# Splitting a low-rank sum in its four groups of partitions, and mixing from two copies of V that transfers within SBUF lay out

## The chip, the cores and the metric

The kernel runs on one core of a Trainium2 chip. Its time is the device time in microseconds (us); three runs of the kernel before the change gave 668.37, 668.86 and 669.84, so the median is 668.86 us. One further execution was recorded with a profile; times inside the kernel come from it, counted from its first instruction.

The core has five engines that run their own instruction streams and wait for each other on semaphores: TensorE (PE for its matmuls, PEld for its weight loads), VectorE (DVE), ScalarE (ACT), GpSimd (POOL) and SyncE (SP). SyncE and ScalarE issue transfers (DMA); the transfers themselves run on 16 DMA engines.

## The reference

An attention with decay and a mixer follow one another. There are B = 4 batches, 768 positions, 8 heads of 64 columns, so 512 channels.

```python
for b in range(nb):                        # blocks of 64 positions
    intra = (q_b @ k_b.T * Dmask) @ v_b
    inter = (q_b * lam_pow) @ kv_state
    out_b = intra + inter
    kv_state = lam_block * kv_state + k_dec.T @ v_b
x = out as (B, 768, 512)
h = x.transpose(0, 2, 1) @ U @ V           # U: 768 x 32, V: 32 x 768
u = x + h.transpose(0, 2, 1)
result = u + maximum(u @ w_ch1, 0) @ w_ch2 # 512 -> 2048 -> 512
```

The part that matters here is h. For one batch, P = U^T x is the low-rank sum, 32 rows (the rank) by 512 channels, summed over all 768 positions. Then u = x + V^T P.

## The kernel before

**Precision.** For the matmuls of the mixer, whose operands have the type float32r, the kernel splits an operand into a high part, which keeps the upper bits of the word (a bitwise and with `HI`), and a low part, the rest. A product of two split operands is the sum of the products of their parts. For V and P it is V_high P_high + V_low P_high + V_high P_low + V_low P_low. Since the rank is only 32, several parts lie one above the other in the 128 partitions, in four groups of 32 (`G` = 4, `R` = 32), and one matmul sums over them.

**The work.** A step s handles 128 positions of one batch; a batch has NT = 6 steps, and there are NS = 24. The list `pieces` (lines 637 to 667) writes out by hand in which order the parts of all steps are issued, and thereby the order on each engine. In a step, `prep` transposes q and k of the next step (and lets SyncE load later ones), `scores`, `intra`, `state` and `inter` are the attention's matmuls, and `aside` issues side work (the conversion of U, V and the first weights from 64-bit words), of which ScalarE's part is put off to `late`.

**The low-rank sum.** After the last step of a batch, `low` (L469) computes P in PSUM: group g of partitions holds the columns g*128 to (g+1)*128, so that pp is 128 partitions by 128 columns. The PSUM buffer is that of px, the attention's output. For the batches 0 to 2, ScalarE (L484) and VectorE (L516) then copy the four groups side by side into the 32 partitions of `p_f` (32 x 512), VectorE takes the high part into `p_h` (L519), ScalarE writes it to its places in `p_hl` (`spread`, L527), GpSimd subtracts for the low part (L531) and ScalarE copies that to its second place (`spread_low`, L538). These last three are the pieces `next_of_low`, issued early in the next step. The last batch, in the product stage, goes its own way.

**V.** `v_hl` holds V's parts as high, low, high, low in the four groups. `v_steps` makes them: ScalarE copies the high part to the groups 0 and 2 (L707), VectorE and GpSimd compute the low part in the groups 1 and 3 (L711).

**The mix.** `mix` (L552) does for one step four matmuls of 64 partitions (two groups) each, L559: for each half of the channels, one with P's high part and one with its low part, each in two groups. The mix of step `done` stands in step s = done + 7; the first in step 7. `mixed` (L571) adds x.

**After.** `turn` transposes u, splits it (L628, L629) and keeps it for the products with w_ch1 (`hidden`, L818 and L828) and, after a pass through DRAM, w_ch2 (L951 to L955), which fill the time from 113 us to the end.

**Transfers and their semaphores.** SyncE issues q, k, the weights' words (L279, L140) and the stores of u (L577) in program order, ScalarE v. A transfer is issued when its buffer is free, and when the earlier transfer that signalled on the same one of eight completion semaphores has landed.

## Time and profile before

| | |
|---|---|
| median of three runs | 668.86 us (668.37 to 669.84) |
| profiled execution, its own time | 665.92 us |
| span from its first to its last instruction | 664.1 us |
| granted TensorE clock | full speed throughout |
| attention stage, up to the first product with w_ch1 | 0 to about 113 us |
| products with w_ch1, then with w_ch2 | 113 to 388, 388 to 664 us |
| a step of attention in the middle of a batch | 4.3 us |
| L484 ScalarE copies of pp, 32x128 | 6, 0.256 us each |
| L516 VectorE copies of pp, 32x128 | 6, 0.288 us each |
| L519 VectorE high part, 32x512 | 3, 0.414 us each |
| L527 and L538 ScalarE copies, 32x256 | 12 and 6, 0.40 us each |
| L531 GpSimd low part, 32x256 | 6, 0.73 us (up to 1.02) each |
| L707 ScalarE copies of V's high part, 32x384 | 4, 0.51 us each |
| L711 V's low part, 32x384 | VectorE 2 (0.55 and 0.99 us), GpSimd 2 (1.00 us each) |
| L559 the mix's matmuls | 72, 0.32 us each |

How to read it: a row's time is from the start of an instruction to its end; weight loads overlap with matmuls, and engines work side by side, so busy times do not add up to the span. A line such as "x4" in the timeline joins instructions of the same kind that follow each other; the time given is then that of all of them. The idle time in brackets is that of the engine before the row, with what released it.

### The profile page before, as it was taken

The page shows a single profiled execution, that of the slowest core. Times are in us where ns is not written, and L with a number is a line of the kernel's source. Part 1 is how long each engine was busy: PE and PEld are TensorE (multiplying, and loading weights), DVE is VectorE, ACT ScalarE, POOL GpSimd, SP SyncE. Part 2 cuts the span into 40 slices and gives each one's busy share as a digit, 9 for nine tenths or more (in the row PEclk, how much of TensorE's full clock was granted, in tenths as well). Part 3 has the DMA queues.
Part 4 walks back from the last instruction along what each step waited for, and adds up shares of the span by engine and source line. Part 5 has one row for each costly group of instructions (what it writes and reads, how often), then busy time and mean ns, then how long its engine had stood idle before and what let it go on. Part 6 is the DMA issues. An engine that isn't in the chain of part 4 may idle for free.

```text
span 664.1 us, 13400 instructions
## 1 busy us (share of the span) xinstructions
PE 655.3 (99%) x5242; PEld 538.9 (81%) x5242; DVE 491.0 (74%) x862; ACT 280.2 (42%) x530; POOL 115.7 (17%) x98
## 2 busy tenths in 40 slices
PE   8999999999999999999999999999999999999997
PEld 8888989888888888888888888888888888888886
DVE  5579989969999777777796256786685775775854
ACT  4777886555555444444453122332322322322220
POOL 4466876330000000000000000030120300300300
PEclk9999999999999999999999999999999999999999
DMA  9999982445867655555578899763363363543521
GB/s 225 256 239 248 246 216 96 150 169 171 278 239 255 212 201 203 202 202 204 199 267 290 310 324 399 249 211 106 95 209 104 116 192 95 175 141 96 172 82 63
DMA packets 131776, 131.29 MB, mean 198 GB/s; under 512 B 81346, under 2 KB 89794, under 8 KB 131714
## 3 DMA queue, kind: packets, MB, share of 16 engines
q1 hardware_dynamic: 106592, 124.02, 58.3%
q10 hardware_dynamic: 25122, 6.42, 4.3%
q8 instruction: 41, 0.67, 0.4%
q14 instruction: 21, 0.17, 0.1%
HBM read 80.09 MB, written 50.33 MB: 196 GB/s over the span
## 4 chain that ended last, share of the span: by engine, by line
PE 94%; DMA 2%; DVE 1%; SPq 1%; ACT 1%; issue 1%; POOL 0%; ACTq 0%; DVEq 0%
PE pz L818 27%; PE pz L953 14%; PE pz L951 14%; PE pd L828 14%; PE pd L955 13%; PE px L447 3%; PE pss L406 3%; PE px L458 2%; PE pqk L358 2%; PE pkv L425 1%; SPq L279 1%; DMA kraw<-in_k_dram 1%; PE pp L474 1%; DMA qraw<-in_q_dram 1%; PE pm L559 1%; PE put L590 1%
## 5 line engine op out<-in xcount | busy, mean ns | idle before, releaser
L818 PE MATMUL pz<-u_hl,w 128*128 128x512 f32 x768 | 190.1, 398 | 0.0
L818 PEld LDWEIGHTS pz<-u_hl,w 128*128 128x128 f32 x768 | 144.2, 189 | 35.0 <-ACT r L824 0.3
L953 PE MATMUL pz<-w_hl,m 128*128 128x512 f32 x384 | 151.1, 397 | 0.0
L951 PE MATMUL pz<-w_hl,m 128*128 128x512 f32 x384 | 151.0, 397 | 0.0
L955 PE MATMUL pd<-w_d,m 128*128 128x512 f32 x384 | 149.5, 397 | 0.0
L934 ACT ACTIVATE m<-mt 128x512 fp32r<-128x512 f32 x96 | 60.6, 632 | 196.8 <-PE pd L955 137.8
L935 DVE SCALAR_TENSOR_TENSOR m<-rm,m 128x512 fp32r<-128x512 f32 x96 | 71.4, 746 | 52.5 <-ACT m L934 52.2
L980 POOL TENSOR_TENSOR o<-o,u 128x512 f32<-128x512 f32 x20 | 29.8, 1522 | 447.4 <-DVE o L976 447.4
L833 DVE SCALAR_TENSOR_TENSOR r<-pd,r 128x512 f32<-128x512 f32 x96 | 61.8, 686 | 53.3 <-ACT r L824 43.5
L828 PE MATMUL pd<-u_d,w 128*128 128x512 f32 x384 | 98.6, 397 | 0.0
L824 ACT ACTIVATE r<-pz 128x512 f32<-128x512 f32 x96 | 52.1, 596 | 92.7 <-PE pz L818 92.6
L953 PEld LDWEIGHTS pz<-w_hl,m 128*128 128x128 f32 x384 | 72.4, 189 | 17.6
L951 PEld LDWEIGHTS pz<-w_hl,m 128*128 128x128 f32 x384 | 72.4, 188 | 17.6
L955 PEld LDWEIGHTS pd<-w_d,m 128*128 128x128 f32 x384 | 72.4, 189 | 17.5
L828 PEld LDWEIGHTS pd<-u_d,w 128*128 128x128 f32 x384 | 72.2, 189 | 17.2
L936 DVE SCALAR_TENSOR_TENSOR m<-m 128x512 fp32r<-128x512 f32 x96 | 69.0, 721 | 0.9
L933 DVE TENSOR_SCALAR mt<-rm 128x512 uint32<-128x512 uint32 x96 | 46.1, 481 | 28.5 <-DMA rm<-r_d 28.2
L415 DVE TENSOR_TENSOR sm<-pss,mask 128x512 f32<-128x512 f32 x48 | 30.9, 684 | 8.0 <-PE pss L406 7.6
L212 ACT CAST w<-wt 128x512 fp32r<-128x512 f32 x32 | 19.9, 620 | 30.6 <-DVE wt L209 23.4
L447 PE MATMUL px<-vraw,sm 128*64 128x64 f32 x768 | 27.9, 225 | 2.4 <-ACT x_nat L464 0.7
L447 PEld LDWEIGHTS px<-vraw,sm 128*64 128x64 f32 x768 | 25.0, 138 | 5.4 <-ACT qt L364 1.8
L406 PE MATMUL pss<-qt,kt 64*128 64x128 f32 x384 | 28.9, 291 | 0.0
(96 smaller groups left out, 667.7 us busy)
## 6 DMA issues: line engine op xcount, KB each, us to landing
r_d<-r SPq DMA_DIRECT2D x96, 256.0 KB, 2.4
rm<-r_d SPq DMA_DIRECT2D x96, 256.0 KB, 2.7
words<-in_moe_w_ch_dram SPq DMA_DIRECT2D x30, 512.0 KB, 4.4
w_d<-w SPq DMA_DIRECT2D x16, 768.0 KB, 3.4
w_hl<-w_d SPq DMA_DIRECT2D x16, 512.0 KB, 6.3
u_d<-x_nat SPq DMA_DIRECT2D x24, 256.0 KB, 3.9
u<-u_d SPq DMA_DIRECT2D x24, 256.0 KB, 4.1
qraw<-in_q_dram SPq DMA_DIRECT2D x23, 256.0 KB, 4.2
```

Source lines behind the costliest of these rows:

```text
L406: nc.tensor.matmul(out=pss[:, x, a, :], lhsT=kt[half[x], a, :], rhs=qt[half[x], a, :], start=True, stop=True,)
L447: nc.tensor.matmul(out=px[half[t], x, a, :], lhsT=sm[:, x, a, half[t]], rhs=vr[:, 2 * a + x, :], start=(a == 0), stop=(alone and a == HP - 1),
L818: nc.tensor.matmul(out=acc[g][0], lhsT=w[:, n, ct, :], rhs=uhl[g][:, n, ct, :], start=(ct == 0 and n == 0), stop=(ct == CT - 1 and n == 1),)
L824: nc.scalar.mul(rs[g], acc[g][0], 4096.0 + 1.0)
L828: nc.tensor.matmul(out=acc[g][1], lhsT=w[:, 2, ct, :], rhs=ud[g][:, ct, :], start=(ct == 0), stop=(ct == CT - 1),)
L833: nc.vector.scalar_tensor_tensor(rs[g], acc[g][1], 4096.0, rs[g], ALU.mult, ALU.add)
L934: nc.scalar.activation(out=m[:, 0], in_=t, func=AF.Relu)
L935: nc.vector.scalar_tensor_tensor(m[:, 1], r, 0.0, hi, ALU.max, ALU.subtract)
L936: nc.vector.scalar_tensor_tensor(m[:, 2], hi, E, low, ALU.mult, ALU.subtract)
L951: nc.tensor.matmul(out=pz, lhsT=m[:, 0, cols], rhs=hl[:, 0], start=first, stop=False)
L953: nc.tensor.matmul(out=pz, lhsT=m[:, 1, cols], rhs=hl[:, 1], start=False, stop=end)
L955: nc.tensor.matmul(out=pd, lhsT=m[:, 2, cols], rhs=dd, start=first, stop=end)
```

## The change

*Low-rank sum.* For the batches 0 to 2, one VectorE copy takes pp as it lies, 128 partitions by 128 columns, to SBUF, and one operation takes the high part. ScalarE then copies the high part of each group to its place (four copies of 32x128), and GpSimd subtracts for the low part of each group (four of 32x128). Nothing is stored twice: `p_hl` becomes a tile of its own with 256 columns. Its groups are: high part of the columns 0 to 255, low part of the same, high part of the columns 256 to 511, low part of the same. The third piece of `next_of_low` is gone for these batches.

*V.* Since P's parts lie only once, V lies in two orders: copy 0 has high, low, high, low in the four groups, copy 1 low, high, low, high. ScalarE writes the high part to group 0 of copy 0, GpSimd the low part to group 1 of copy 0, and six transfers within SBUF, issued by SyncE at the beginning of step 6, before the loads of that step's `prep`, fill the six others (32 partitions by 768 columns of 4 bytes each, 96 KB).

*Mix.* A mix remains four matmuls of 64 partitions by 256 columns; the two that add up now use the two copies of V and the same columns of `p_hl`. The last batch keeps its P in the part of V's second copy that is no longer read by then, and multiplies with copy 0.

*Room.* The one-row tile with lam moves into a part of the tile `blank`, and two constants into `small`.

```diff
@@ -287,11 +287,12 @@
 
     assert G == 4
     vp = w1_pool.tile([P, 3, C], F32R, tag="w1", name="vp").rearrange("p n c -> p (n c)")
-    v_hl, p_hl = vp[:, 0:S], vp[:, S : S + C]
+    v_hl = vp.rearrange("p (n c) -> p n c", n=2)
+    p_hl = consts.tile([P, 2 * P], F32R, name="p_hl")
 
 
     ident = keep.tile([P, P], FP32, name="ident")
-    small = consts.tile([P, 16], FP32, name="small")
+    small = consts.tile([P, 18], FP32, name="small")
     zeros = small[:, 0:1]
 
     mask = consts.tile([P, 2, HP, P], FP32, name="mask")
@@ -464,7 +465,7 @@
         nc.scalar.copy(xs[s].rearrange("p (a x e) -> p x a e", a=HP, x=2), px)
         del st[s]
 
-    pps, others = {}, {}
+    pps = {}
 
     def low(b):
 
@@ -479,17 +480,15 @@
         if b == B - 1:
             pps[b] = pp
             return
-        pps[b] = rows_f = tmp("p_f")[0:R]
-        for g in range(2):
-            nc.scalar.copy(rows_f[:, g * P : (g + 1) * P], pp[g * R : (g + 1) * R])
-        others[b] = pp
+        pps[b] = pp
 
     def low_rows(b):
 
-        pp, t = pps.pop(b), tmp("p_h")[0:R]
+        pp = pps.pop(b)
         own = [(slice(g * R, (g + 1) * R), slice(g * P, (g + 1) * P)) for g in range(G)]
         if b == B - 1:
-            h, h2, l, l2 = (p_hl[g * R : (g + 1) * R] for g in range(G))
+            t = tmp("p_h")[0:R]
+            h, h2, l, l2 = (v_hl[g * R : (g + 1) * R, 1, 0:C] for g in range(G))
             for rows, cols in own:
                 nc.vector.tensor_scalar(
                     t[:, cols].bitcast(U32), pp[rows].bitcast(U32), HI, None, ALU.bitwise_and
@@ -511,33 +510,26 @@
             pps[b] = [spread, low_part, spread_low]
             return
 
-        rows_f, pp = pp, others.pop(b)
-        for g in range(2, G):
-            nc.vector.tensor_copy(
-                out=rows_f[:, g * P : (g + 1) * P], in_=pp[g * R : (g + 1) * R]
-            )
-        nc.vector.tensor_scalar(t.bitcast(U32), rows_f.bitcast(U32), HI, None, ALU.bitwise_and)
-        wide = [slice(x * 2 * P, (x + 1) * 2 * P) for x in range(2)]
+        whole, t = tmp("p_f")[:, 0:P], tmp("p_h")[:, 0:P]
+        nc.vector.tensor_copy(out=whole, in_=pp)
+        nc.vector.tensor_scalar(t.bitcast(U32), whole.bitcast(U32), HI, None, ALU.bitwise_and)
 
         def place(g, low):
-            return p_hl[g * R : (g + 1) * R, wide[low]]
-
-        def spread():
+            n = 2 * (g // 2) + low
+            return p_hl[n * R : (n + 1) * R, (g % 2) * P : (g % 2 + 1) * P]
+
+        def high_part():
             for g in range(G):
-                nc.scalar.copy(place(g, 0), t[:, wide[g // 2]])
+                nc.scalar.copy(place(g, 0), t[g * R : (g + 1) * R])
 
         def low_part():
-            for x in range(2):
+            for g in range(G):
+                rows = slice(g * R, (g + 1) * R)
                 nc.gpsimd.tensor_tensor(
-                    out=place(2 * x, 1), in0=rows_f[:, wide[x]], in1=t[:, wide[x]],
-                    op=ALU.subtract,
-                )
-
-        def spread_low():
-            for x in range(2):
-                nc.scalar.copy(place(2 * x + 1, 1), place(2 * x, 1).bitcast(FP32))
-
-        pps[b] = [spread, low_part, spread_low]
+                    out=place(g, 1), in0=whole[rows], in1=t[rows], op=ALU.subtract
+                )
+
+        pps[b] = [high_part, low_part]
 
     def next_of_low(b):
         pps[b].pop(0)()
@@ -551,19 +543,18 @@
 
     def mix(s):
         b, c = divmod(s, NT)
-        weights = v_hl[:, c * P : (c + 1) * P]
+        weights = v_hl[:, :, c * P : (c + 1) * P]
         if b < B - 1:
             pm = both_halves(s)[:, :, 2 * P :]
-            for low in range(2):
+            for n in range(2):
                 for x in range(2):
                     nc.tensor.matmul(
-                        out=pm[:, x], lhsT=weights[half[x]],
-                        rhs=p_hl[half[x], low * 2 * P : (low + 1) * 2 * P],
-                        start=(low == 0), stop=(low == 1),
+                        out=pm[:, x], lhsT=weights[half[x], n], rhs=p_hl[half[x]],
+                        start=(n == 0), stop=(n == 1),
                     )
             return
         pu = bank([P, C], "pu", "b2")
-        nc.tensor.matmul(out=pu, lhsT=weights, rhs=p_hl, start=True, stop=True)
+        nc.tensor.matmul(out=pu, lhsT=weights[:, 0], rhs=v_hl[:, 1, 0:C], start=True, stop=True)
         nc.vector.tensor_tensor(out=xs[s], in0=pu, in1=xs[s], op=ALU.add)
 
     def mixed(s):
@@ -642,7 +633,7 @@
         turns = done > 0 and (done - 1) // TG < FG
         mixes = 0 <= done < NS - NT - 1
         rows = c == 0 and b > 0
-        step = [("prep", s + 1)] * more
+        step = [("spread_v", s)] * (s == NT) + [("prep", s + 1)] * more
         step += [("turn", done - 1)] * turns + [("mix", done)] * mixes
         step += [("mix", done + 1)] * (not more)
         step += [("next_of_low", b - 1)] * rows + [("next_of_low", b - 1)] * rows
@@ -652,7 +643,6 @@
         step += [("turned", done - 2)] * (done > 1 and c == 1)
         step += [("split", done - 1)] * turns
         step += [("mixed", done)] * mixes + [("mixed", done + 1)] * (not more)
-        step += [("next_of_low", b - 1)] * rows
         both = [("intra", s), ("state", s)]
         step += (both if s > NT else both[::-1]) + [("next_v", s), ("inter", s)]
         step += [("late", s)] * (s < 2 or s in (NT - 1, NT))
@@ -689,11 +679,10 @@
                 st["v"] = wconv.tile([P, C], FP32, tag="wf", name="vf")[0 : 2 * R, 0:SH]
             return st["v"]
 
-        def parts(gs):
+        def parts(g):
             for half in range(2):
                 rows, cols = slice(half * R, (half + 1) * R), slice(half * SH, (half + 1) * SH)
-                for g in gs:
-                    yield v_hl[g * R : (g + 1) * R, cols], rows
+                yield v_hl[g * R : (g + 1) * R, 0, cols], rows
 
         def five():
             st["t"] = t = wconv.tile([P, C], FP32, tag="wt", name="vt")[0 : 2 * R, 0:SH]
@@ -703,18 +692,28 @@
             on_scalar(high)
 
         def high():
-            for out, rows in parts((0, 2)):
+            for out, rows in parts(0):
                 nc.scalar.copy(out, st["t"][rows])
 
-        def low(g, engine):
-            for out, rows in parts((g,)):
-                engine.tensor_tensor(
+        def low():
+            for out, rows in parts(1):
+                nc.gpsimd.tensor_tensor(
                     out=out, in0=st["v"][rows], in1=st["t"][rows], op=ALU.subtract
                 )
 
+        def spread():
+            whole = v_hl.bitcast(FP32)
+            for g, n in ((2, 0), (1, 1), (3, 1), (3, 0), (0, 1), (2, 1)):
+                source = (g + n) % 2
+                nc.sync.dma_start(
+                    out=whole[g * R : (g + 1) * R, n],
+                    in_=whole[source * R : (source + 1) * R, 0],
+                )
+
+        run["spread_v"] = lambda s: spread()
         halves = [moe_V[:, half * SH : (half + 1) * SH] for half in range(2)]
         return weight_steps(dst, halves, SH, 2 * R, in_parts=True) + [
-            five, lambda: low(1, nc.vector), lambda: low(3, nc.gpsimd),
+            five, low,
         ]
 
 
@@ -724,7 +723,7 @@
     side = {}
     for steps, at in (
         (u_side, (-1, 1, 1, 2, 2)),
-        (v_steps(), (0, 0, 3, 3, 4, 4, 4, 5, 5)),
+        (v_steps(), (0, 0, 3, 3, 4, 4, 4, 5)),
         (w1_steps(0, True), (3, 4, 5, 6, 8, 9, 10, 11, 13, 14, 15)),
         (w1_steps(1, True, True), (8, 9, 10, 11, 16, 17, 19, 20, 21, 22, 23, NS)),
     ):
@@ -745,11 +744,11 @@
 
     ordered = ctx.enter_context(ExitStack())
     ordered.enter_context(tc.manual_schedule())
-    lam_row = consts.tile([1, H + P], FP32, name="lam_row")
-    blank = x_pool.tile([P, C], FP32, tag="x", name="blank")[:, 0:P]
+    blank = x_pool.tile([P, C], FP32, tag="x", name="blank")
+    lam_row, blank = blank[0:1, P : P + H + P], blank[:, 0:P]
     nc.vector.memset(blank, 0.0)
     nc.vector.memset(lam_row[:, H:], 1.0)
-    set_ends(vp[:, S + C : S + C + 2].bitcast(FP32))
+    set_ends(small[:, 16:18])
     nc.scalar.dma_start(out=lam_row[:, 0:H], in_=lam.unsqueeze(0))
     load_next("q", nc.sync)
     load_next("k", nc.scalar)
```

## The prediction

> **What bounds the kernel now.** I read the page first, for the engine that sets the time.
>
> ```profile
> span 664.1 us, 13400 instructions
> ...
> PE 655.3 (99%) x5242; PEld 538.9 (81%) x5242; DVE 491.0 (74%) x862; ACT 280.2 (42%) x530; POOL 115.7 (17%) x98
> ...
> PE 94%; DMA 2%; DVE 1%; SPq 1%; ACT 1%; issue 1%; POOL 0%; ACTq 0%; DVEq 0%
> ```
>
> TensorE carries 94% of the chain that ended last. The change touches only the attention stage (up to 113 us) and leaves the number and shape of matmuls as they are, so it can give or take only stretches in which TensorE stands still there. The table by stage finds them (columns: stretch, its length, then busy us and count of PE, PEld, DVE, ACT, POOL, clock, DMA share, GB/s).
>
> ```profile
> 33.00:41.00 8.00, 7.20 (x172) 6.15 (x172) 6.22 (x11) 6.88 (x17) 5.60 (x7) 1.00 0.96 226
> ...
> 60.00:67.00 7.00, 6.75 (x174) 6.00 (x172) 6.07 (x13) 5.29 (x13) 3.99 (x5) 1.00 0.88 220
> ...
> 88.00:94.00 6.00, 5.81 (x154) 5.17 (x154) 5.00 (x10) 4.40 (x12) 3.78 (x4) 1.00 0.75 186
> ...
> 142.00:388.00 246.00, 246.00 (x1052) 197.87 (x1051) 185.61 (x334) 113.75 (x198) 1.30 (x1) 1.00 0.66 230
> ```
>
> After 113 us there is no TensorE gap until 388, so time won or lost before 113 should reach the end one to one. The three short stretches are where a batch's low-rank sum is split. There I read the timeline; in brackets is how long the engine stood idle before, and what ended it. First batch, weight loads and ScalarE:
>
> ```profile
> 37.15 1.66 ACT L527 CAST vp<-p_h 32x256 fp32r<-32x256 f32 x4
> 38.83 0.83 ACT L538 CAST vp<-vp 32x256 fp32r<-32x256 f32 x2
> 39.29 0.18 PEld L559 LDWEIGHTS pm<-vp 64*128 64x128 f32 x1 [0.18 <-ACT vp L538]
> 39.69 0.58 ACT L464 COPY x_nat<-px 128x512 f32<-128x512 f32 x1
> 39.71 0.18 PEld L559 LDWEIGHTS pm<-vp 64*128 64x128 f32 x1 [0.24 <-ACT vp L538]
> ```
>
> The first mix waits for the last of ScalarE's copies, and the next step's attention product, whose weight load starts at 40.32 after 0.43 us idle, waits for x_nat, which stood behind those copies. Second and third batch:
>
> ```profile
> 62.94 0.59 DVE L516 COPY p_f<-pp 32x128 f32<-32x128 f32 x2 [0.79 <-PE pqk L358]
> 63.60 1.04 PEld L447 LDWEIGHTS px<-vraw,sm 128*64 128x64 f32 x32 [0.36 <-ACT qt L364]
> 65.94 0.42 DVE L431 COPY kv<-pkv 128x256 f32<-128x256 f32 x1
> 66.41 0.33 PEld L358 LDWEIGHTS pqk<-ident,qraw 64*128 64x128 f32 x8 [0.26 <-DVE kv L431]
> ```
>
> ```profile
> 90.80 1.04 PEld L447 LDWEIGHTS px<-vraw,sm 128*64 128x64 f32 x32 [0.30 <-issue]
> 91.73 0.58 PEld L425 LDWEIGHTS pkv<-vraw,ks 128*64 128x64 f32 x16
> 92.38 0.97 PEld L406 LDWEIGHTS pss<-qt,kt 64*128 64x128 f32 x16
> 93.61 0.33 PEld L358 LDWEIGHTS pqk<-ident,qraw 64*128 64x128 f32 x8 [0.26 <-DVE kv L431]
> ```
>
> The 0.36 is put down to qt, but px shares its PSUM buffer with pp, and L516, the last reader of pp, ended at 63.53, 0.07 before the weight load; in the third batch it ended at 90.73, 0.07 before 90.80. So I read both as waits for L516. The 0.26 is a wait for kv, which stands on VectorE behind L516, L519 and three operations on u.
>
> **What the Trainium skill says.** "VectorE: DVE Perf Modes", The perf-mode tier table: fp32 tensor_scalar from SBUF runs at two elements a cycle; with the roughly 150 cycles of start that the page gives beside its modes, 512 columns make 406 cycles, 0.42 us. The trace has 0.414 for L519, so I use it for 128 columns: 214 cycles, 0.22 us. "SBUF — State Buffer", Door 1: 32 partitions reach 8 of 16 DMA ports, 189 GB/s measured at 1 MiB; 96 KB would take 0.52 us, an estimate. Here the two V loads of the same shape landed 0.37 us apart, in a full queue. "DMA: Bandwidth & Descriptors", Anatomy: about 2 us fixed per transfer. In this trace the quickest are the last stores (1.8 us, 128 KB) and a first q load (2.4 us); no transfer within SBUF is in it.
>
> **The change part by part.**
>
> *Low-rank sum, three batches.* ScalarE loses two copies of 0.26 (L484), four of 0.415 (L527) and two of 0.41 (L538), and gains four of 32x128. 32x384 takes 0.51 and 32x256 0.40, so 128 columns less are 0.10, and 32x128 costs 0.30, about 1.25 for four: 3.0 becomes 1.25. VectorE: 0.59 and 0.41 become one copy of 128x128 (0.29: the 32x128 copy's time, since 64x384 at 0.35 against 128x512 at 0.41 shows that columns count) and 0.22. GpSimd: two of 0.73 become four of 0.45 (1.00 for 384 columns, 0.73 for 256, so 0.27 per 128): 0.4 us more. Cover: qs, the next thing on GpSimd, is read a step of 4.3 us later; without it the 0.4 would be paid.
>
> Second batch: VectorE copies pp as soon as it is done and its engine free (62.27), ending at 62.6, before the mix's last weight load ends (63.24): the 0.36 goes. p_h is done at 62.85, the first operation on u waits for its transposes (63.2), kv comes 0.8 earlier: the 0.26 goes. What is late next is nothing: scores and kt stand ready. Third batch the same, 0.30 and 0.26. Together 1.18 us. The mix now waits on GpSimd directly; low parts there can start when the previous batch's last mix has read p_hl (63.45) and end at 65.4; the mix stands at 66.6.
>
> *First batch.* High copies end at 38.4 instead of 39.66 and x_nat at 39.0; qt and kt follow, so the 0.18, 0.24 and 0.43 (0.85 together) have no ScalarE cause left. The scores' mask on VectorE (38.64, two of 0.65) is ready for the product at 39.3.
>
> *V.* ScalarE's four copies (2.07) become two, VectorE's two subtractions at 36.23 (1.55) go, GpSimd keeps two. All lay beside TensorE work: nothing on the path. The rows that were computed in place now come by six transfers on SyncE, ahead of the next q, k and weight loads.
>
> ```profile
> 30.60 1.44 SPq L279 DMA_DIRECT2D kraw<-in_k_dram  x1
> 31.40 0.38 ACTq L279 DMA_DIRECT2D vraw<-in_v_dram  x1
> 32.09 1.37 SPq L140 DMA_DIRECT2D words<-in_moe_w_ch_dram  x1
> ...
> 35.73 0.37 SPq L279 DMA_DIRECT2D qraw<-in_q_dram  x1
> ```
>
> SyncE idles from 33.46 to 35.73. The first three transfers wait for V's high copies (33.6), the fourth for GpSimd (34.26); at 0.4 us each, four are issued by about 35.3. In the compiled order each transfer also waits for the earlier one that used its completion semaphore, one of eight in turn: the fifth waits for the k load of 30.60, which the trace has landing at 37.04, the sixth for the v load of 31.40 (36.14). So the fifth goes at 37.1 and the sixth at 37.45. With nothing else on SyncE's queue (DMA moved 57 to 75 GB/s from 36 to 37) I take 2.05 us, between the 1.8 and the 2.4 above: the sixth lands at 39.5. The mix (38.86) needs the fifth for its third and the sixth for its fourth matmul. Fourth weight load 39.55 instead of 39.71, attention product 39.75 instead of 40.32: 0.57 of the 0.85 is won. Bounds: 1.8 us gives 0.8; 4.5 us, the median of a k load under load here, lands at 41.95 and loses 1.9.
>
> Behind them q goes at 37.9 instead of 35.73, k at 38.3, the weights at 38.8 (36.78). Each is read at least two steps, some 8 us, later and takes 4.2 to 4.5 to land; SyncE waited for TensorE again at 43.98, so it has caught up by then. Without that cover q would delay a step by 2.
>
> *Moves of lam_row and the two constants, last batch's rows in V's second copy:* same instructions in the same places; nothing.
>
> Sum: 0.57 + 0.62 + 0.56 = 1.75 us. On the profiled execution, 665.92 with a span of 664.1 and 1.8 around it, that makes 664.2 and 662.35. The median of the runs, 668.86, is 2.9 above it; I take the difference off that: 667.1.
>
> **Rivals.** *Late spread, slower.* At the first mix the sixth transfer takes as long as a load in this stage does. Break-even with the 1.18 of the later batches is an attention product at 41.5, a landing at 41.3, 3.9 us after issue. At 4.5 us the net is 0.6 slower (669.5), at the 6.8 of the slowest k load 3 slower (671.8). For: the queue's share is 0.96 in this stretch, and fewer ports. Against: SyncE's own block empties the queue. 0.15.
>
> *Half a gain.* The 0.36 and 0.30 belong to what the profile names, or an instruction-fetch wait ("issue", 0.66 at 35.43) returns with the loads now bunched at 38 to 41: 0.7 to 1.1 won, 668.0. For: bracketed names. Against: the 0.07 us in both batches. 0.27.
>
> *Whole gain.* The k load lands earlier and the first mix waits for nothing: 0.85 + 1.18 and a little, 666.6. 0.13.
>
> The forecast itself: 0.45, its own range 666.6 to 667.6.
>
> **Numbers.** 0.2% (1.3 us, below 667.5) is about what a measurement tells from no change. Faster: most of the forecast (0.42) and the whole gain, 0.55. Same: 0.03 of the forecast, half a gain, little of the late spread: 0.31. Slower: 0.14. The range 665.9 to 669.6 takes in all but the late spread's tail and part of the whole gain's.
>
> **What would show it.** After: no idle before L447's weight load in the steps after a pp, none before pqk for kv; six transfers issued between 33.6 and 37.9 with a gap before the fifth; the first mix's fourth weight load between 39.2 and 40, released by a transfer. It is wrong if that load stands after 41, if the low parts on GpSimd take over 3 us, or if the time won by 113 us is lost before 388.

## The result, and the profile after

The changed kernel takes 670.62 us, the median of 20 runs (668.16 to 673.84). The kernel before, run beside it, takes 668.85 us (666.62 to 671.15). The ratio is 1.0030, with an interval of 1.0017 to 1.0043: the change makes the kernel about 1.8 us slower. The forecast was 667.1 us, 1.75 us faster, with a range up to 669.6.

The page of the changed kernel: span, busy time of each engine, and the chain that ended last.

```profile
span 668.0 us, 13401 instructions
...
PE 657.0 (98%) x5242; PEld 540.9 (81%) x5242; DVE 487.8 (73%) x857; ACT 273.8 (41%) x516; POOL 115.8 (17%) x104
...
PE 96%; DMA 1%; issue 1%; DVE 1%; ACT 0%; POOL 0%; ACTq 0%; DVEq 0%; POOLq 0%
```

The other engines changed as the diff says: five VectorE and fourteen ScalarE instructions fewer, six on GpSimd more. TensorE is busy 1.7 us longer with the same 5242 matmuls, the first sign that some of them ran slower. The table by stage (columns as in the prediction: stretch, length, then busy us and count of PE, PEld, DVE, ACT, POOL, clock, DMA share, GB/s):

```profile
33.00:41.00 8.00, 5.37 (x141) 4.70 (x132) 3.28 (x7) 5.17 (x14) 6.21 (x8) 1.00 0.89 217
41.00:60.00 19.00, 18.44 (x480) 17.30 (x481) 13.84 (x24) 11.13 (x27) 9.44 (x8) 0.91 1.00 246
...
88.00:94.00 6.00, 6.00 (x178) 5.41 (x176) 5.21 (x10) 3.60 (x8) 3.59 (x3) 1.00 0.98 252
142.00:388.00 246.00, 246.00 (x1054) 197.84 (x1053) 184.35 (x331) 114.52 (x198) 2.60 (x2) 1.00 0.67 231
```

In the third batch (88 to 94) TensorE has no gap left, as predicted. In the first batch (33 to 41) it is busy for 5.37 us instead of 7.20, and in the stretch behind it the mean granted clock is 0.91. From 142 to 388 TensorE is busy throughout in both kernels. The timeline around the first mix, from SyncE's issues (SPq) and TensorE:

```profile
32.48 2.83 SPq L140 DMA_DIRECT2D words<-in_moe_w_ch_dram  x1
...
35.40 4.37 SPq L708 DMA_DIRECT2D vp<-vp  x6
...
38.23 0.19 PEld L551 LDWEIGHTS pm<-p_hl,vp 64*128 64x128 f32 x1
...
41.53 0.74 PEld L551 LDWEIGHTS pm<-p_hl,vp 64*128 64x128 f32 x3 [3.11 <-issue]
41.56 1.00 PE L551 MATMUL pm<-p_hl,vp 64*128 64x256 f32 x3 [2.94 <-DMA vp<-vp]
42.49 1.78 PEld L448 LDWEIGHTS px<-vraw,sm 128*64 128x64 f32 x32 [0.22 <-issue]
42.50 1.97 PE L448 MATMUL px<-vraw,sm 128*64 128x64 f32 x32
```

The first of the four mix matmuls needs no transferred rows and starts at 38.26. The second needs the first and the fourth transfer, of which the fourth landed at 41.32, and stands until 41.53: the transfers, not ScalarE's copies, now hold the mix. (The brackets of the weight loads name "issue" here and GpSimd in other runs below; the landings tell which transfer it was.) Behind it the product px takes 1.97 us, where the same 32 matmuls take 1.15 us in the other steps. The two windows that the profile's clock record marks:

```profile
38.20:41.61 3.41, 0.47 (x12) 0.30 (x6) 1.10 (x2) 2.29 (x7) 2.27 (x3) 1.00 0.83 215
41.61:45.02 3.41, 3.41 (x51) 3.19 (x51) 0.69 (x1) 0.00 (x0) 0.00 (x0) 0.50 1.05 250
```

TensorE was idle for 2.9 of 3.41 us, and in the next 3.41 us it was granted half its clock. The kernel before had no such stretch before its last 0.2 us.

To compare executions I take three segments from the starts of weight loads: from one batch's low-rank sum (pp) to the next, and from the third to the first product with w_ch1. In the kernel before they are 27.74, 27.26 and 25.67 us. The table gives the difference to these in the one profiled execution, and the ratio of the runs' times to those of the kernel before, run beside them. (The ratio is an estimate from all runs, and differs by up to 0.6 parts in a thousand from the quotient of the two medians.) The runs are described below.

| | ratio and 95% interval | span | pp 1 to 2 | pp 2 to 3 | pp 3 to product |
|---|---|---|---|---|---|
| changed kernel | 1.0030 (1.0017 to 1.0043) | 668.0 | +3.61 | +0.37 | −0.29 |
| e1 first mix reads no V | 0.9989 (0.9974 to 1.0003) | 664.3 | +0.32 | −0.15 | −0.29 |
| e2 no transfers | 0.9978 (0.9966 to 0.9989) | 662.0 | −1.47 | −0.83 | −0.30 |
| e3 words later | 1.0026 (1.0015 to 1.0037) | 665.9 | +1.78 | −0.13 | −0.30 |
| e4 wait filled | 1.0024 (1.0013 to 1.0035) | 667.7 | +2.51 | +0.93 | −0.31 |
| e5 four transfers | 1.0025 (1.0009 to 1.0041) | 668.1 | −0.03 | +0.35 | −0.29 |
| e10 the same again | 1.0026 (1.0012 to 1.0041) | 666.5 | +2.66 | −0.06 | −0.30 |
| e6 mix moved | 0.9995 (0.9982 to 1.0009) | 663.8 | −0.17 | −0.84 | −0.30 |
| e7 moved, words later | 0.9982 (0.9968 to 0.9995) | 663.8 | −0.88 | −0.84 | −0.30 |
| e11 the same again | 0.9989 (0.9975 to 1.0002) | 663.4 | +0.21 | −0.84 | −0.29 |
| e8 all three | 0.9996 (0.9985 to 1.0007) | 664.9 | −0.37 | +1.35 | −0.30 |
| e9 V a step earlier | 1.0030 (1.0013 to 1.0046) | 667.9 | −1.06 | +0.80 | −0.30 |
| e12 before, words later | 1.0004 (0.9992 to 1.0016) | 666.8 | −0.10 | +2.30 | 0.00 |

A span is one execution. The last row shows how far one can stand from the median: e12 is 2.7 us longer than the kernel before in the profile, and not told from it in 22 runs. The profiled execution of the changed kernel is nearly 4 us longer, where the medians differ by 1.8. Where the two differ, the ratio counts, and the profile only tells the place.

### The profile page after: what moved, and what is told of

Same layout as the page of the kernel before. It is cut to its first block, busy times and chain, and to the rows that moved or that the text cites. A ratio compares the mean times of both kernels' runs of the same rounds, so it can differ in the third digit from the quotient of the medians.

```text
span 668.0 us, 13401 instructions
## 1 busy us (share of the span) xinstructions
PE 657.0 (98%) x5242; PEld 540.9 (81%) x5242; DVE 487.8 (73%) x857; ACT 273.8 (41%) x516; POOL 115.8 (17%) x104
## 4 chain that ended last, share of the span: by engine, by line
PE 96%; DMA 1%; issue 1%; DVE 1%; ACT 0%; POOL 0%; ACTq 0%; DVEq 0%; POOLq 0%
PE pz L817 27%; PE pz L952 13%; PE pd L827 13%; PE pz L950 13%; PE pd L954 13%; PE px L448 4%; PE pss L407 4%; PE px L459 2%; PE pqk L359 2%; PE pkv L426 1%; PE pp L475 1%; PE pm L551 1%; DMA kraw<-in_k_dram 1%; PE pm L599 1%; PE put L581 1%
## 5 line engine op out<-in xcount | busy, mean ns | idle before, releaser
L416 DVE TENSOR_TENSOR sm<-pss,mask 128x512 f32<-128x512 f32 x48 | 30.9, 684 | 10.6 <-PE pss L407 10.6
L448 PE MATMUL px<-vraw,sm 128*64 128x64 f32 x768 | 29.5, 232 | 1.8 <-issue 0.9
```

The lines of the kernel that those rows point to most:

```text
L448: nc.tensor.matmul(out=px[half[t], x, a, :], lhsT=sm[:, x, a, half[t]], rhs=vr[:, 2 * a + x, :], start=(a == 0), stop=(alone and a == HP - 1),
```

## The experiments

Theory A: the loss is the wait for late transfers at the first mix, and the half clock behind it. Theory B: the loss is the transfers' traffic, the loads that they push back, or the split on GpSimd, wherever the mix stands.

**e1, the first mix reads no V.** The first step's mix takes `p_hl` as its weights, so the right addend of that step is left out; the transfers are issued all the same.

```diff
-                        out=pm[:, x], lhsT=weights[half[x], n], rhs=p_hl[half[x]],
+                        out=pm[:, x], lhsT=p_hl[half[x], 0:P] if s == 0 else weights[half[x], n], rhs=p_hl[half[x]],
```

> The changed kernel, but the first mix (step 0 only) takes the low-rank sum itself as weights in place of V, so that it waits for no transfer; the six transfers stay as they are, and V is first needed a step of 4.3 us later. What step 0 adds is therefore left out. Theory A (the wait for the late transfers is the loss: 3.1 us of idle TensorE and about 1.3 us of half clock behind it, together 4.4): about 666.2 us against 670.6 of the change, and below the kernel before by 2 to 2.7. Theory B (the transfers cost by their traffic, by pushing other loads back, or the split on GpSimd costs): not below the kernel before, 668.9 or more.

Measured: 0.9989. The wait and the half clock are gone, and with them 4 parts in a thousand. But a new wait stands two steps later. Timeline of e1, VectorE and TensorE:

```profile
46.30 0.43 DVE L160 TENSOR_SCALAR sc<-words 128x512 uint32<-128x512 uint32 x1 [0.74 <-DMA words<-in_moe_w_ch_dram]
...
46.64 1.53 DVE L149 TENSOR_SCALAR m<-words 128x512 uint32<-128x512 uint32 x1
...
48.09 1.27 DVE L416 TENSOR_TENSOR sm<-pss,mask 128x512 f32<-128x512 f32 x2
...
48.84 1.13 PEld L448 LDWEIGHTS px<-vraw,sm 128*64 128x64 f32 x32 [1.57 <-ACT kt L365]
```

The words of the weights, pushed back behind the six transfers, landed at 46.28. VectorE's conversion of the words waits for them (0.74 us), the mask of the scores (L416) follows it in VectorE's program, and the attention product, which needs the mask, waits 1.57 us. The bracket names kt, but kt had ended at 48.10, while the first of the two mask operations, 0.68 us each, ended at about 48.77, just ahead of px. Not all of this is the words' lateness: VectorE stood idle for 0.74 us, and then the conversion's second instruction (L149) took 1.53 us, where it takes 0.41 in the kernel before, in the changed kernel and in e6. A GpSimd instruction of 1.28 us began just ahead of it, at 46.61; whether that stretched it, no run here shows. So B is partly right: a pushed-back load can start a wait of 1.57 us, but only when the first wait no longer hides it.

**e2, no transfers.** V's tile is zeroed at the start and six of its eight blocks are left out; everything else is the changed kernel.

```diff
-        run["spread_v"] = lambda s: spread()
+        run["spread_v"] = lambda s: None
...
+    nc.gpsimd.memset(vp.bitcast(FP32), 0.0)
```

> The changed kernel without the six transfers; V's tile is set to zero at the start on an idle GpSimd, so six of the eight blocks of V's two copies are left out of the sum. Theory A: as the run with the first mix freed, 666.2 within 0.5 us. Theory B in the form of traffic: at least 1 us below that run, as the waits for nothing that the profile shows (0.71 and 0.60 us at 67 and 77 us) go with the transfers. B in the form of the split: 669 or more here too.

Measured: 0.9978, the segments −1.47, −0.83 and −0.30. Without the transfers the split, the copies and the mix from two orders gain 2.2 parts in a thousand, 1.5 us, near what the prediction said of them. Taking out the transfers takes out the whole loss, so it is not in the split, and GpSimd's four parts cost nothing that shows. The median is 0.6 us below that of e1, more than A allowed (0.5) and less than B's traffic asked for (1); the two intervals overlap.

**e3, the words behind the transfers.** One fetch of words on SyncE moves from step 5 to step 6, so that it no longer stands ahead of the transfers.

```diff
-        (w1_steps(0, True), (3, 4, 5, 6, 8, 9, 10, 11, 13, 14, 15)),
+        (w1_steps(0, True), (3, 4, 6, 6, 8, 9, 10, 11, 13, 14, 15)),
```

> The changed kernel, but the weights' words that SyncE issues just ahead of the transfers (2.8 us of its time, until 35.3) are issued behind them. Theory A: first transfer at 33.3 instead of 35.4, sixth issued at about 37.3 when the k load has landed, landed by 40.2 instead of 41.9; TensorE idle 1.7 instead of 3.1 us, no half clock: 668 us, between the kernel before and 667. Theory B: 670.6, as the transfers are the same.

Measured: 1.0026. The transfers are issued from 33.50 to 38.26 instead of 35.40 to 39.76 and the last lands at 40.14 instead of 41.88. Weight loads of the first mix in e3:

```profile
39.02 0.18 PEld L551 LDWEIGHTS pm<-p_hl,vp 64*128 64x128 f32 x1 [0.85 <-POOL qs L391]
...
39.89 0.18 PEld L551 LDWEIGHTS pm<-p_hl,vp 64*128 64x128 f32 x1 [0.68 <-DMA vp<-vp]
40.24 0.18 PEld L551 LDWEIGHTS pm<-p_hl,vp 64*128 64x128 f32 x1 [0.17 <-issue]
```

The wait falls from 3.11 to 1.70 us, which is 1.4 of the 1.8 us won in this segment. The first bracket names GpSimd, but the fourth transfer landed at 38.81, 0.21 us ahead of that weight load. The half clock is there again, from 41.65 on. The ratio can't be told from that of the changed kernel, although the landing and the wait came out as A expected. Even with SyncE free in time the transfers are not back in time, since each takes 2.5 to 3.8 us from the start of its issue to its landing, and the six issues 4.8 us together.

**e4, the wait filled.** Eight 128x128 matmuls of the identity with itself go ahead of the first mix, into a part of its PSUM buffer that nothing reads.

```diff
+            for i in range(8 * (s == 0)):
+                nc.tensor.matmul(
+                    out=both_halves(s)[:, 0, 0:P], lhsT=ident, rhs=ident, start=True, stop=True
+                )
```

> The changed kernel with eight matmuls of no use (128x128, into a part of the mix's PSUM buffer that is not read) ahead of the first mix, which fill most of TensorE's wait of 3.1 us. They can gain nothing by themselves. If the wait costs more than its own length because the granted clock halves behind it (3.4 us at half clock, attention products 1.97 instead of 1.15): about 1.3 us less than the change, 669.3, and no stretch at half clock. If the clock is not part of the loss: 670.6 or more.

Measured: 1.0024, no stretch of half clock. Timeline of e4:

```profile
38.65 2.05 PE L550 MATMUL pm<-ident 128*128 128x128 f32 x16
...
41.68 0.31 PEld L555 LDWEIGHTS pm<-p_hl,vp 64*128 64x128 f32 x2 [0.87 <-POOL qs L391]
...
42.49 1.15 PE L448 MATMUL px<-vraw,sm 128*64 128x64 f32 x32
```

px stands at 42.49, as in the changed kernel (42.50), but takes 1.15 us, and the next scores start 2.17 us after it instead of 3.30. So the half clock cost 1.1 us in that execution. The times of the runs don't show this gain: the ratios differ by 0.6 parts in a thousand, well inside the intervals, and the medians, against the kernel before, not at all (1.9 and 1.8 us slower). How much of the loss is the half clock is thus open.

That the stretch comes with a wait can be seen in the mean granted clock of each run. A stretch of 3.41 us at half clock takes 0.0026 off the mean (an estimate: half of 3.41 over 668), so a run that has one should show 0.997 or less. Of the changed kernel's 20 runs 13 do, with a median of 671.0 us; the other seven have 669.6, but a run with a longer wait may have both. Of the runs of the kernel before for which the record gives the clock, 1 of 200 does. In e4 it is none of 20, in e1, e2, e8 and e11 none either, in e7 and e12 1 of 22 each; in e3 7 of 17, in e5 and e10 6 and 9 of 22, in e9 9 of 11 (in the profiles of e5 and e9 the wait and the stretch lie earlier, between 20 and 29 us).

**e5 and e10, four transfers.** Two of the four carry 64 partitions, the bytes are the same.

```diff
-            for g, n in ((2, 0), (1, 1), (3, 1), (3, 0), (0, 1), (2, 1)):
-                source = (g + n) % 2
+            for g, n, source, count in ((2, 0, 0, 2), (1, 1, 0, 2), (0, 1, 1, 1), (3, 1, 0, 1)):
                 nc.sync.dma_start(
-                    out=whole[g * R : (g + 1) * R, n],
-                    in_=whole[source * R : (source + 1) * R, 0],
+                    out=whole[g * R : (g + count) * R, n],
+                    in_=whole[source * R : (source + count) * R, 0],
                 )
```

> The changed kernel, with the six transfers of 32 partitions made four by letting two of them carry 64 partitions (the same bytes). If the time of a transfer's issue and its landing count per transfer (theory A), two issues of 0.7 us fall away, the last lands near 40.6 instead of 41.88, the first mix waits some 1.2 us less, and the ratio to the kernel before falls from 1.003 to about 1.001 (to 0.999 if the stretch of half clock goes too). If the bytes count (theory B), or 64 partitions take longer to land, the wait stays near 3 us and the ratio stays at 1.003.

Measured: 1.0025. The profiled execution had lost 3.4 us ahead of the change, most of it to one wait of 2.77 us that ended at 23.2 and the half clock behind it; as the mix stood later for that reason, the transfers were nearly in time for it (0.61 us of wait). That says nothing on an ordinary execution. The same kernel again:

> The version with four transfers once more, since the profiled execution of its first run lost 3.4 us to a stretch of half clock at 24.6 us, ahead of the change, and so does not show its wait at the first mix. Theory A: in an execution without that early loss the last transfer lands some 1.2 us earlier than with six, and the first mix still waits 1.5 to 2 us; ratio 1.001 to 1.0025. Theory B: the wait is the 3 us of the changed kernel, and the ratio 1.003.

Measured: 1.0026. Weight loads of the first mix in e10:

```profile
38.90 0.18 PEld L551 LDWEIGHTS pm<-p_hl,vp 64*128 64x128 f32 x1 [0.75 <-POOL qs L391]
...
40.78 0.30 PEld L551 LDWEIGHTS pm<-p_hl,vp 64*128 64x128 f32 x2 [1.70 <-issue]
```

The wait is 2.45 us instead of 3.11, so 0.66 of the 1.2 us expected was won: there are two issues fewer, but one of the four took 1.95 us, and landing took 3.2 to 5.0 us from the issue instead of 2.7 to 3.8. The half clock is there again, from 41.49. The ratio doesn't tell this from six transfers.

**e6, the first mix moved.** Mix and addition of the first step go behind the attention products of the same step (2.3 us of TensorE work); nothing else is changed.

```diff
-        step += [("turn", done - 1)] * turns + [("mix", done)] * mixes
+        step += [("turn", done - 1)] * turns + [("mix", done)] * (mixes and done > 0)
...
-        step += [("mixed", done)] * mixes + [("mixed", done + 1)] * (not more)
+        step += [("mixed", done)] * (mixes and done > 0) + [("mixed", done + 1)] * (not more)
...
         step += (both if s > NT else both[::-1]) + [("next_v", s), ("inter", s)]
+        step += [("mix", 0), ("mixed", 0)] * (done == 0)
```

> The changed kernel, with the first mix alone moved behind the attention products of its own step, so that 2.4 us of TensorE work stand between the transposes and it; transfers and loads as in the changed kernel. Theory A (the loss is the wait for the late transfers and the half clock behind it): the wait shrinks from 3.1 to some 0.7 to 0.9 us, no half clock, 3.5 us won, ratio about 0.997 to 0.998. Theory B (the loads pushed back by the transfers cost as much by themselves): the scores' mask of the next step waits for the pushed-back words as it did when the first mix read no transfer, 1.5 us of it come back, ratio 0.999 to 1.000.

Measured: 0.9995, 3.5 parts in a thousand (2.3 us) below the changed kernel, with intervals that do not overlap. Timeline of e6:

```profile
34.03 5.10 SPq L709 DMA_DIRECT2D vp<-vp  x6
...
42.41 0.30 PEld L551 LDWEIGHTS pm<-p_hl,vp 64*128 64x128 f32 x4
```

The last transfer landed at 41.51, the mix started at 42.41 and waited for nothing; this execution has no half clock. Transfers and loads are all there and only their reader stands later, so the wait at the first mix, with what follows it, made up the loss against the kernel before. The ratio itself lies in the range that B had asked for, but not for B's reason: the conversion of the words no longer delays the mask as it did in e1 (VectorE reaches it at 47.32, after the words have landed at 45.85). What keeps e6 from the 0.9978 of e2 is in part open. The wait for x_nat (see e7) is in it, and 4 of the 22 runs still have a mean clock of 0.997 or less, with a median of 668.7 us against 665.9 for the other 18; where these lose it, no trace shows.

**e7 and e11, mix moved and words later.**

> First mix moved behind its step's attention products, and the words' fetch of step 5 moved to step 6, behind the transfers, so that the transfers are issued from 33.5 on as predicted and land by 40.1. Theory A: no wait is left at the first mix (it stands near 40.9), span about 2 us below the kernel before, ratio 0.997. Theory B: the words land later still (near 46.5), VectorE's conversion waits for them and holds the scores' mask back, ratio 0.999 to 1.001.

Measured: 0.9982. Timeline of e7, SyncE and weight loads:

```profile
34.69 3.77 SPq L709 DMA_DIRECT2D vp<-vp  x6
...
40.25 1.12 PEld L448 LDWEIGHTS px<-vraw,sm 128*64 128x64 f32 x32 [0.46 <-ACT x_nat L465]
...
42.54 0.30 PEld L551 LDWEIGHTS pm<-p_hl,vp 64*128 64x128 f32 x4
```

The mix runs its four matmuls in one go. What is late next is px, for x_nat, by 0.46 us: the kernel before had a wait of 0.43 us for it here, and with the mix gone from in front of px nothing hides it. The ratio lies between what A and B expected. Once more:

> The version with the first mix moved and the words behind the transfers once more, to see whether it beats the kernel before. Theory A: ratio 0.997 to 0.999 with an upper end below 1. Theory B: 0.9995 to 1.001, the first result having been luck.

Measured: 0.9989, with an interval that just reaches 1. The two ratios say 1.2 and 0.7 us faster than the kernel before, the medians 0.9 and 0.4; one of the two intervals excludes no change, the other doesn't. And since this version carries the words' new place, the kernel before got it alone (e12, the diff of e3 on the old kernel):

> The kernel before, with nothing but the words' fetch of step 5 moved to step 6. If what the moved-mix version wins over the kernel before comes from the change's split of the sum and the transfers once they are in time (theory A), this makes no difference: ratio 0.9995 to 1.0005. If it comes from fetching the words later, with the change having no part in it (theory B), ratio 0.998 to 0.999. If the words land too late for VectorE's conversion here too, ratio 1.001 or more.

Measured: 1.0004 (0.9992 to 1.0016). The words' place is worth nothing that shows by itself. The kernel before was not run with its first mix moved. Its own mix waits 0.18 and 0.24 us for ScalarE's copies, so up to 0.4 us of what e7 and e11 win could come from the move alone; that is not tested.

**e8, all three.** Four transfers, mix moved, words later.

> Four transfers, first mix moved, words behind the transfers. If both parts of the loss are understood, this comes to what the kernel without transfers showed: ratio 0.998, span 662.0 to 662.5, no half clock, no wait at the first mix; SyncE is free for q, k and words some 1 to 1.5 us earlier than with six transfers, so the scores' mask waits at most 0.5 us for words. If the transfers cost by their traffic in a way that neither the count nor the place touches, it stays at 0.9995 to 1.001.

Measured: 0.9996. No wait at the first mix and no half clock, as expected, but no better than with six transfers: the ratio lies where the expectation put a cost of the traffic itself, and that cost stays neither shown nor excluded. In its profile the second batch is 1.35 us longer, with four waits of 0.29 to 0.48 us that are put down to nothing ("issue"). Such waits come without the change too: e12 has four in its second batch, from 0.32 to 1.15 us. So I don't count them for or against four transfers.

**e9, V a step earlier.** Conversion, copies and transfers of V move ahead by a step; the mix stays.

```diff
-        (v_steps(), (0, 0, 3, 3, 4, 4, 4, 5)),
+        (v_steps(), (0, 0, 2, 2, 3, 3, 3, 4)),
...
-        step = [("spread_v", s)] * (s == NT) + [("prep", s + 1)] * more
+        step = [("spread_v", s)] * (s == NT - 1) + [("prep", s + 1)] * more
```

> The changed kernel, with the conversion of V, its two copies and subtractions and the six transfers each one step (4.3 us) earlier; the first mix stays where it is, and so do the words. Theory A (the transfers come too late for the first mix, and nothing else is wrong with them): they are issued from about 30 on and have landed by 37, ahead of the mix near 38.5; no wait there, no half clock, pp to pp in the first batch 0.5 to 1.5 us shorter than before, ratio 0.997 to 0.999. Theory B (their traffic and the loads behind them cost as much wherever they stand): q and k of the next steps land later and the scores of step 6 or 7 wait 1 to 2 us, ratio 1.001 to 1.003.

Measured: 1.0030, outside what A expected and inside what B did. Timeline of e9, in step 2 and at the first mix:

```profile
22.25 0.35 DVE L160 TENSOR_SCALAR sc<-words 64x384 uint32<-64x384 uint32 x1 [1.49 <-DMA words<-in_moe_V_dram]
...
22.90 1.50 DVE L178 SCALAR_TENSOR_TENSOR m<-words,m 64x384 f32<-64x384 uint32 x1
...
24.33 1.27 DVE L416 TENSOR_TENSOR sm<-pss,mask 128x512 f32<-128x512 f32 x2
...
25.12 1.82 PEld L448 LDWEIGHTS px<-vraw,sm 128*64 128x64 f32 x32 [3.55 <-ACT sc L168]
...
41.89 0.31 PEld L551 LDWEIGHTS pm<-p_hl,vp 64*128 64x128 f32 x4
```

The first mix waits for nothing, and its segment is 1.06 us shorter than before: what A says of that place is right. But the loss came back elsewhere. V's own words had not landed when VectorE reached them (1.49 us idle), one instruction of the conversion took 1.50 us where it takes 0.55 in the kernel before, the mask stood behind both, and TensorE waited 3.55 us, with half clock from 24.8. It is the chain of e1 again, and not that of q and k which B named.

## Why the prediction was wrong

**The step that failed: the landing of the sixth transfer in the part on V.** I let SyncE be free at 33.46, took 0.4 us for each issue and 2.05 us from issue to landing, and made the fifth wait for a k load. All three terms were too small, and the wait that I put in cost nothing. From the view of the line that issues them:

```profile
L708 SPq DMA_DIRECT2D vp<-vp x6: 540/594/1165, 35.4 to 39.2; - x6
...
DMA to landing us min/median/max: 2.7/3.1/3.8
```

- SyncE was free at 35.30. The words' issue ahead of the transfers took 2.83 us instead of 1.37. That an issue's time varies was to be read from the profile before: its three issues of w_ch1 words near this place took 1.84, 0.97 and 1.37 us.
- The six issues took 4.37 us instead of some 2.4. I had argued that SyncE's queue would be empty when they came; it was not: v, q, k and words landed at 35.55, 36.37, 37.28 and 38.19 (the share of the DMA engines was 0.89 from 33 to 41).
- Landing took 2.7 to 3.8 us (five of the six have a recorded landing) instead of 2.05. The Trainium skill, "DMA: Bandwidth & Descriptors", Anatomy of one DMA, has about 2 us of fixed cost, and has it for transfers that GpSimd issues; for these of SyncE, 2.7 us was the least. A 96 KB transfer within SBUF was in no trace before; it should have been priced from transfers under the same load and not from the quickest ones of the trace.
- The fifth was issued at 38.54, later than the k load's landing (37.28). That wait cost nothing.

Together the last landing is 41.88 instead of 39.5. My break-even of 3.9 us from issue to landing was counted from an issue at 37.45; counted from the real 39.18, it was 41.3 − 39.18 = 2.1 us, and none of the recorded landings was that quick.

**The rival that came true** is "late spread, slower", to which I gave 0.15 and 669.5 to 671.8 us; the median is 670.62. Its price lacked the half clock. For a landing at 41.95 I had the attention product at about 42.2 and a loss of 0.6 us. It stood at 42.50, and then ran at half speed. The kernel before, from its first mix to the next scores, and the same stretch a step later:

```profile
38.86 0.24 PEld L559 LDWEIGHTS pm<-vp 64*128 64x128 f32 x2
...
42.54 0.97 PEld L406 LDWEIGHTS pss<-qt,kt 64*128 64x128 f32 x16
...
44.22 0.31 PEld L559 LDWEIGHTS pm<-vp 64*128 64x128 f32 x4
...
46.84 0.97 PEld L406 LDWEIGHTS pss<-qt,kt 64*128 64x128 f32 x16
```

and the scores behind the changed kernel's first mix, which starts at 38.23:

```profile
45.80 0.97 PEld L407 LDWEIGHTS pss<-qt,kt 64*128 64x128 f32 x16
```

The kernel before takes 3.68 us, 1.06 more than a step later, where nothing waits (2.62). The changed kernel takes 7.57: the 2.62, the wait of 3.11, 1.14 us more from px to the scores, at half clock, and 0.70 for the mix's last matmuls, which cross into the half clock, and the gap of 0.22 ahead of px.

**The first batch's gain was right, and hidden.** From pp to the first mix the changed kernel is 0.27 us quicker, no more than the difference of an "issue" wait ahead of it (0.39 us instead of 0.66). The gain lies behind that, at the waits of 0.18, 0.24 and 0.43 us for ScalarE's copies, and there the wait for the transfers covers it. e2, without that wait, has none of the three and shows the segment at −1.47; 0.66 of this is the "issue" wait of the kernel before, which e2 happens not to have, so some 0.8 us are the change's, near the 0.85. One part is not general: when the mix moves away (e6, e7) the wait for x_nat is back.

**The split: sizes right.** VectorE's copy takes 0.29 us and the high part 0.23 (predicted 0.29 and 0.22), ScalarE's four high copies 1.21 together (1.25), GpSimd's four parts 2.00 (four of 0.45, 1.8). The waits before px that I read as waits for the copy of pp are gone (in e7 too), and none before pqk is put down to kv. "Half a gain" was right on one point: "issue" waits of 0.71 and 0.60 us stand in the second batch of the changed kernel. Such waits are in e4 as well (0.52 and 0.28), not in e2, e6, e7 or e11 (−0.83 to −0.84), but in e12 without the change. What makes them is open.

**The third batch gave 0.30, not 0.56.** The step that failed is that I added up idle times of the weight-load row. TensorE's matmul row in the same stretch, before:

```profile
90.23 0.48 PE L559 MATMUL pm<-vp 64*128 64x256 f32 x4
90.83 1.15 PE L447 MATMUL px<-vraw,sm 128*64 128x64 f32 x32
...
92.38 1.16 PE L406 MATMUL pss<-qt,kt 64*128 64x128 f32 x16
93.61 0.47 PE L358 MATMUL pqk<-ident,qraw 64*128 64x64 f32 x8
```

and after:

```profile
93.84 0.48 PE L551 MATMUL pm<-p_hl,vp 64*128 64x256 f32 x4
94.25 1.15 PE L448 MATMUL px<-vraw,sm 128*64 128x64 f32 x32
95.80 1.16 PE L407 MATMUL pss<-qt,kt 64*128 64x128 f32 x16
96.86 0.47 PE L359 MATMUL pqk<-ident,qraw 64*128 64x64 f32 x8
```

From mix to px it is 0.60 before and 0.41 after; from scores to transposes 1.23 and 1.06. That is 0.36 us, not 0.56, and 0.30 of it reach the first product. A weight load that doesn't wait still starts some 0.1 us behind the one before it: the mix's four loads take 0.31 us and its four matmuls 0.48, and px, which waits for nothing there, is loaded at 94.25, 0.13 us after them. The second batch gave 0.84 where nothing was lost to "issue", more than the 0.62 predicted: by the same reckoning the two gaps gave 0.25 and 0.17 there (e7), and the rest is a wait of 0.43 us for qt, at 76.49 in the kernel before, which went too. e12, without the change, doesn't have it either, so that part is not the change's: luck of the one execution.

**What went right:** time is decided by 113 us. The first product with w_ch1 is 3.33 us late in the profile, and the shift stays within 0.1 us until the last product with w_ch2. Loads behind the transfers were covered as predicted for q and k, but not the words: I followed who reads q and k, and took the words as two steps off without asking what stands behind their conversion on VectorE. e1 shows that it is the scores' mask, and e9 shows the same for V's words.

## What to carry to other kernels

A transfer that replaces engine copies has to be placed by its queue: count when the issuing engine is really free, take issue and landing times from transfers under the same load, and put the first reader behind other work if the sum comes near. Here the same change is 1.8 us slower than the kernel before with one mix ahead of 2.3 us of TensorE work, and not told from it with that mix behind (e6); with one fetch moved as well it was 0.4 to 1.2 us faster (e7, e11). When work is moved to an earlier or a later place, follow on every engine what stands behind its wait.

## What the runs showed of the hardware

A wait on TensorE can cost more than its length: px took 1.97 us behind the wait of the changed kernel, and 1.15 where e4 filled it. The Trainium skill, "TensorE: Matmul & The Clock Gate", Part 1: The HAM clock gate, says that a free-running window of 3413 ns decides between full and half clock, and that half comes after at least one idle window. The traces agree on the length (each stretch is 3.41 us, and the full-speed stretches recorded ahead of it, 30.72 us in the changed kernel, e3 and e10 and 13.65 us in e5 and e9, are nine and four times that) and on the two values, 1.0 and 0.5. They differ on "idle": windows in which TensorE was busy for 10%, 14%, 38% and 42% of the time (e9, the changed kernel, e10, e5) were followed by half clock, and in e3 one with 66%:

```profile
38.24:41.65 3.41, 2.24 (x40) 1.65 (x41) 1.51 (x3) 2.14 (x6) 2.48 (x3) 1.00 1.02 250
41.65:45.06 3.41, 3.41 (x64) 3.17 (x62) 0.42 (x1) 0.59 (x1) 1.06 (x1) 0.50 1.10 270
```

Windows of 59%, 61% and 66% in e1, e7 and e2, counted in steps of 3.413 us from the clock record, were not. So in e3 waits of 1.70 us together were enough, while windows as empty or emptier were not followed by half clock. Where the limit lies, and whether busy time is the right measure of it, these runs leave open. Unexpected too was how much one kind of issue on SyncE can vary: the four for words between 25 and 42 us took from 0.87 to 2.83 us in the changed kernel.
